# A convolution's taps moved from VectorE to ScalarE and accumulating DMA transfers, in a gated matmul kernel on one core

## The chip, the core and the metric

The kernel runs on one core of a Trainium2 chip. The metric is the device time of one execution in microseconds (us). A profile of one execution names the engines as PE (TensorE, with PEld for its weight loads), DVE (VectorE), ACT (ScalarE), POOL (GpSimd) and SP (SyncE, which here only issues DMA transfers).

## What is computed

```python
# x (8, 4096, 192), weight (8, 7), w_in (192, 2048), w_out (2048, 192), all float32
w = softmax(weight, axis=-1)                   # 8 heads of 24 columns, 7 taps
x_pad = concatenate([zeros(B, 6, D), x], axis=1)
conv[b, s, col] = sum_k w[head(col), k] * x_pad[b, s + k, col]
h = conv.reshape(32768, 192) @ w_in
g = h * (1 / (1 + exp(-1.702 * h)))
out = g @ w_out                                # (32768, 192)
```

## The kernel before

**Batches and steps.** The eight sequences are two halves of four. A batch (`big`, 0 to 31) is 512 tokens of one sequence of each half. It lies with 64 rows of d_model on the lower 64 partitions for the batch's first 256 tokens and on the upper 64 for the second 256. Each batch is done in two steps s = 2 big and s = 2 big + 1, 64 steps in all. Steps 0 and 1 are written out (`first_step`, `second_step`), steps 2 to 63 are one loop of `hidden`, `give`, `output`.

**What a batch needs beforehand (`prepare`, L432).** `transpose_x` (L385) has DVE turn the loaded tile xin into xt, three instructions. `load_x` (L103) then loads the next batch's x by eight transfers on SP's queue. `conv` multiplies each of three chunks c of 64 columns by its seven taps k: k = 0 is a multiply (L400), k = 1 to 6 a multiply-add onto f (L402), all on DVE over 128x512. `sums_c` (L310, L312) makes eight sums V1 to V8 of the chunks' quarters, because the products follow a fast scheme that multiplies sums. `cross` (L410) copies f to the other 64 partitions (`crossed`) by DMA on SP's queue: for the even step in three parts (V1 and its neighbour first, 128 KB; the quarters, 256 KB; V2 to V8, 448 KB), for the odd step in one of 832 KB.

**Where that work stands.** `prepare` yields pieces with an estimated time. They wait in the list `todo`, and calls of `work(us)` at fixed places in `hidden` and `output` take as many of them as fit, so that DVE does them between what PE and ACT wait for. `need(label)` takes all up to a label. Each engine works through its instructions in the order in which the program writes them.

**A step.** `hidden` (L490) makes 21 terms of the first matmul by `product1` (L457: 64 rows by 128 columns, 256 tokens) in four PSUM tiles: `sums` and the slots x, z and y. ACT copies some partial sums out into five SBUF tiles `kept` of 128x1024, called k15, k16, k19, k18 and k20 (L498, L503, L509, L511, L517), DVE adds and subtracts, and ACT applies the gelu (L473) into g. `fetch` puts term 16 of the next step into z ahead of the last two terms of this one; it needs V1 and its crossing. `output` (L603) makes the products p1, p2, p6, p5 and p7 by `product2` (L547, 64 matmuls each, 128 rows by 32 columns) and four short ones (L563). Between them ACT copies results out of PSUM (L611 and L612 after p1, L618 after p2, L624 after p6, L631 and L633 after p5, L640 after p7). DVE makes sums of g (L483) and of the results, and turns them (L581), and SP stores them (L596). While `output` runs, all five `kept` tiles are free.

**Buffers that matter.** f has two buffers, xin and xt one each, `kept` five that live for the whole run. The slots are PSUM tiles of two banks: a bank can be written again once its readers are done.

Of the kernel before, what the change touches and what calls it, by code (L numbers as in the profile page):

```python
# [15 lines left out]
def kernel(  # L16
# [73 lines left out]
    def load_x(big):  # L90


        p, c = divmod(big, CHUNKS)
        xin = xins[big] = xin_pool.tile([P, 2, NJ, XW], F32, name="xin")
        if c == 0:
            nc.gpsimd.memset(xin[0:R, :, 0, :], 0.0)
        for n in range(2):
            for o in range(2):
                j = 1 if c == 0 and o == 0 else 0
                t = c * TOK + o * T + (j - 1) * Q  # L100
                for v in range(2):
                    q0 = o * R + v * Q
                    nc.sync.dma_start(  # L103
                        out=xin[q0 : q0 + Q, n, j:NJ, :],
                        in_=x_v[n, p, t : t + (NJ - j) * Q, v * Q : v * Q + XW].rearrange(
                            "(j i) d -> i j d", i=Q
                        ),
                    )
# [272 lines left out]
    def transpose_x(big, c, n=None):  # L381
        if big not in xts:
            xts[big] = xt_pool.tile([P, NC, 2, XT], F32, name="xt")
        ns = slice(0, 2) if n is None else slice(n, n + 1)
        vec.transpose(  # L385
            xts[big][:, c, ns, :].rearrange("p n (j t) -> p (n j) t", t=Q),
            xins[big][:, ns, :, :].rearrange("p n j d -> p (n j) d")[:, :, c * R : c * R + Q],
        )
        if c == NC - 1 and n != 0:
            xins.pop(big)  # L390

    def conv_src(big, c, k, ns=slice(0, 2)):
        return xts[big][:, c, ns, Q - PAD + k : Q - PAD + k + T]
# [12 lines left out]
    def sums_c(big, i):  # L406
        add_up(lambda j: fs[big][:, j, :], *SUMS_C[i])
# [12 lines left out]
    def cross_even(*what):  # L420
        if given[0] < what[0] - 1:
            waiting.append(what)
        else:
            cross(what[0], 0, *what[1:])
# [7 lines left out]
    def prepare(big):  # L432

        for c in range(NC):
            yield "", 0.7, lambda c=c: transpose_x(big, c)
        if big + 1 < N_BIG:
            yield "", 0.0, lambda: load_x(big + 1)
        yield "", 0.0, lambda: new_f(big)

        for c in (0, 2):  # L440
            for k in range(K):
                yield "", 0.76 if k else 0.48, lambda c=c, k=k: conv(big, c, k)
        yield "", 0.38, lambda: sums_c(big, 0)
        yield f"first {big}", 0.0, lambda: cross_even(big, V1, C32 + 1)
        for k in range(K):
            yield "", 0.76 if k else 0.48, lambda k=k: conv(big, 1, k)
        yield "", 0.0, lambda: cross_even(big, 0, V1)
        for i in range(1, len(SUMS_C)):
            yield "", 0.38, lambda i=i: sums_c(big, i)
        yield f"all {big}", 0.0, lambda: cross_even(big, C32 + 1, NB)  # L450

    def product1(slot, a, b, s, first=False):
        f, o = fs[s // 2], s % 2
        for j in range(2):
            for h in range(2):

                nc.tensor.matmul(  # L457
                    slot[:, h, j * T : (j + 1) * T],
                    w_in_s[halves[h], a, j * P : (j + 1) * P],
                    (f if h == o else crossed)[halves[h], b, :],  # L460
                    start=(first and j == 0),
                    stop=True,
                    skip_group_check=True,
                )
# [14 lines left out]
    def sum_g(u, dst):  # L479
        j = NK // 2 * u  # L480
        v = [g[:, b, j : j + NK // 2, :] for b in range(NS)]
        a, b = {T1: (B12, B11), T2: (B22, T1), T3: (B22, B12), T4: (T2, B21)}[dst]
        vec.tensor_sub(v[dst], v[a], v[b])  # L483
# [6 lines left out]
    def hidden(s, x, z, y, work, fetch):  # L490

        k15, k16, k19, k18, k20 = kept

        def pe(slot, *ts, first=False):
            terms(s, slot, *ts, first=first)

        pe(sums, 12)
        act.copy(k15, sums)  # L498
        pe(x, 5, 17)
        gelu(B11, 0, x)  # L500
        pe(z, 7, first=True)
        pe(sums, 0)
        act.copy(k16, sums)  # L503
        work(1.5)
        pe(y, 6, 14, first=True)
        vec.tensor_sub(x, z, k15)
        work(2.6)
        pe(sums, 13)
        act.copy(k19, sums)  # L509
        pe(x, 2)  # L510
        act.copy(k18, x)  # L511
        pe(z, 11)
        pe(sums, 20, 10)
        vec.tensor_sub(k15, y, k19)  # L514
        gelu(B12, 0, sums)
        pe(x, 4)
        act.copy(k20, x)  # L517
        vec.tensor_sub(k19, z, k19)
        work(1.1)
        gelu(B22, 1, k19)  # L520
        gelu(B22, 0, k15)
        pe(y, 8)
        pe(sums, 1, 9, first=True)
        pe(y, 15)
        sum_g(0, T1)
        work(1.1)
        vec.tensor_add(k20, k20, sums)  # L527
        vec.tensor_sub(k16, y, k16)
        gelu(B11, 1, k20)
        pe(x, 18)  # L530
        gelu(B21, 1, x)
        gelu(B21, 0, k16)
        sum_g(0, T2)
        fetch()
        pe(sums, 3, 19)
        work(0.7)
        vec.tensor_add(k18, k18, sums)  # L537
        gelu(B12, 1, k18)
        work(1.1)
# [60 lines left out]
    def chunk(t, c):  # L600
        return t[c * Q : (c + 1) * Q, :]

    def output(s, ra, rb, work, between=None):  # L603

        out = Out(s)
        u1, u2, p3, p4 = (
            u_pool.tile([NC * Q, T], F32, name=f"u{i}") for i in range(4)
        )

        p1, p3c = product2(ra, 0, (A11, B11), (S4, B22, 0))  # L610
        act.copy(u1, p1)  # L611
        act.copy(chunk(p3, 0), p3c)  # L612
        sum_g(1, T1)
        sum_g(1, T2)
        sum_g(1, T4)
        sum_g(0, T4)
        p2, p3c = product2(rb, 0, (A12, B21), (S4, B22, 1))
        act.copy(chunk(p3, 1), p3c)  # L618
        vec.tensor_add(u2, u1, p2)  # L619
        out.turn(0, 0, u2)  # L620
        sum_g(0, T3)
        sum_g(1, T3)
        p6, p3c = product2(ra, 1, (S2, T2), (S4, B22, 2))
        act.copy(chunk(p3, 2), p3c)  # L624
        vec.tensor_add(u2, u1, p6)
        work(4.2)
        if between:
            between()
        p5, p4c = product2(rb, 1, (S1, T1), (A22, T4, 0))
        q = quarters(rb, 0, A22, T4, 2)  # L630
        act.copy(chunk(p4, 0), p4c)  # L631
        vec.tensor_add(u1, u2, p5)
        act.copy(chunk(p4, 2), q[2])  # L633
        vec.tensor_add(p3, u1, p3)
        out.turn(0, 1, p3)
        for l in (0, 1, 3):
            vec.tensor_add(chunk(p4, 2), chunk(p4, 2), q[l])
        work(1.5)
        p7, p4c = product2(ra, 0, (S3, T3), (A22, T4, 1))
        act.copy(chunk(p4, 1), p4c)  # L640
        vec.tensor_add(u1, u1, p7)
        vec.tensor_add(u2, u2, p7)
        out.turn(1, 1, u1)
        vec.tensor_sub(u2, u2, p4)
        out.turn(1, 0, u2)
        out.store()
# [143 lines left out]
    def second_step(fetch):  # L790

        quarters = [
            (0, 0, slots[2], B11), (1, 0, sums, B21), (1, 1, slots[0], B22), (0, 1, slots[1], B12)
        ]
        for u in range(2):
            for i, (m, n, slot, b) in enumerate(quarters):
                plain(1, u, m, n, slot)
                gelu(b, u, slot)
                if u == 1 and i < 2:
                    sum_g(0, (T1, T2)[i])  # L800
                work(2.5)
        todo.extend(("", 0.42, lambda i=i: sums_w_in(i)) for i in range(FREE, len(SUMS_W)))
        todo.append(("sums", 0.0, lambda: None))
        todo.extend(prepare(2))
        output(1, slots[0], slots[1], work, fetch)
        need("all 1")
        cross(1, 1)
        need("sums")
# [4 lines left out]
    def fetch(s, slot):  # L813

        need(f"first {s // 2}")
        terms(s, slot, 16, first=True)
# [8 lines left out]
    second_step(fetch_2)  # L825
    for s in range(2, N_ST):
        more = s + 1 < N_ST
        hidden(s, x, z, y, work, lambda: fetch(s + 1, z) if more else None)
        give(s)
        if more:  # L830
            begin(z)
        if s % 2 and (s + 3) // 2 < N_BIG:
            todo.extend(prepare((s + 3) // 2))
        output(s, y, x, work)
        if s % 2 and more:
            need(f"all {(s + 1) // 2}")
            cross((s + 1) // 2, 1)
        x, z = z, x
# [30 lines left out]
```

## Time and profile before

| | |
|---|---|
| time, median of 3 runs | 2382.21 us (2382.08 to 2382.79) |
| span of the profiled execution | 2380.8 us, 71620 instructions |
| multiply-adds of taps (L402) on DVE, 128x512 | 558, 747 ns each, 416.9 us |
| first taps (L400) on DVE, 128x512 | 93, 466 ns each, 43.4 us |
| turning of x (L385) on DVE, 128x576 | 93, 744 ns each, 64.8 us |
| copies to k15, k16, k19 (ACT, 128x1024) | 62 of each, 1012 ns each |
| copies of 32 or 96 rows by 256 in the output (ACT) | 364 to 369 ns |
| copies of 128x512 from PSUM (ACT, at the start) | 592 and 586 ns |
| transfers on SP's queue | 131.06 MB, 28.2% of 16 engines' time |
| transfers issued by POOL | one, 0.13 MB |

A line of the page's fifth part, or of the list of groups, gives line, engine, operation, output and input tiles, shapes and count; then the busy time, the mean of one, and the idle time of the engine just before with what ended it. A line of the timeline gives start and length in us, engine and line, and in brackets the wait before it. A line of the DMA issues gives the queue, the count, the size of one and the time from issue to landing. In the granted clock PE has full speed all the time.

### The profile page before, as it was taken

The page shows a single profiled execution, that of the slowest core. Times are in us where ns is not written, and L with a number is a line of the kernel's source. Part 1 is how long each engine was busy: PE and PEld are TensorE (multiplying, and loading weights), DVE is VectorE, ACT ScalarE, POOL GpSimd, SP SyncE. Part 2 cuts the span into 40 slices and gives each one's busy share as a digit, 9 for nine tenths or more (in the row PEclk, how much of TensorE's full clock was granted, in tenths as well). Part 3 has the DMA queues.
Part 4 walks back from the last instruction along what each step waited for, and adds up shares of the span by engine and source line. Part 5 has one row for each costly group of instructions (what it writes and reads, how often), then busy time and mean ns, then how long its engine had stood idle before and what let it go on. Part 6 is the DMA issues. An engine that isn't in the chain of part 4 may idle for free.

```text
span 2380.8 us, 71620 instructions
## 1 busy us (share of the span) xinstructions
PE 2371.0 (100%) x32598; PEld 1748.3 (73%) x32598; DVE 2038.6 (86%) x2855; ACT 1051.4 (44%) x1363; POOL 9.0 (0%) x30
## 2 busy tenths in 40 slices
PE   9999999999999999999999999999999999999998
PEld 6777777777777777777777777777777777777776
DVE  8898988888888889888898888898888988889865
ACT  5345344344453443444534434445344344453443
POOL 1000000000000000000000000000000000000000
PEclk9999999999999999999999999999999999999999
DMA  7323323223233132331232322323313233123120
GB/s 165 71 50 58 65 53 66 48 42 69 50 68 59 30 68 56 62 65 36 56 67 52 66 51 41 69 50 67 59 30 68 58 61 66 39 52 68 25 42 15
DMA packets 195983, 136.02 MB, mean 57 GB/s; under 512 B 110784, under 2 KB 186176, under 8 KB 193696
## 3 DMA queue, kind: packets, MB, share of 16 engines
q1 hardware_dynamic: 194912, 131.06, 28.2%
q8 instruction: 255, 4.18, 0.7%
q10 hardware_dynamic: 720, 0.26, 0.1%
q14 instruction: 48, 0.39, 0.1%
q0 software_dynamic: 48, 0.13, 0.0%
HBM read 53.15 MB, written 25.17 MB: 33 GB/s over the span
## 4 chain that ended last, share of the span: by engine, by line
PE 99%; DMA 1%; ACT 0%; DVE 0%; SPq 0%; issue 0%; ACTq 0%; DVEq 0%
PE slot L547 47%; PE slot L457 28%; PE sums L457 21%; PE slot L563 2%; DMA g<-in_moe_w_in_dram 0%; DMA crossed<-f 0%; SPq L103 0%; DVE f L291 0%; ACT f L281 0%; ACT kept L281 0%; ACT f L280 0%; ACT kept L280 0%; ACT f L282 0%; DVE osb L581 0%; SPq L227 0%
## 5 line engine op out<-in xcount | busy, mean ns | idle before, releaser
L547 PE MATMUL slot<-g,w_out_s 128*32 128x256 f32 x20544 | 1133.5, 379 | 0.0
L547 PEld LDWEIGHTS slot<-g,w_out_s 128*32 128x32 f32 x20544 | 661.0, 110 | 451.2 <-issue 20.9
L457 PE MATMUL slot<-f,w_in_s 64*128 64x256 f32 x3120 | 724.7, 376 | 0.0
L457 PE MATMUL slot<-crossed,w_in_s 64*128 64x256 f32 x3120 | 724.6, 376 | 0.0
L483 DVE TENSOR_TENSOR g<-g 128x1024 f32<-128x1024 f32 x504 | 602.5, 1215 | 82.3 <-ACT g L473 77.0
L457 PEld LDWEIGHTS slot<-crossed,w_in_s 64*128 64x128 f32 x3120 | 583.1, 187 | 35.7 <-issue 0.4
L457 PEld LDWEIGHTS slot<-f,w_in_s 64*128 64x128 f32 x3120 | 583.1, 187 | 34.1 <-issue 0.8
L457 PE MATMUL sums<-crossed,w_in_s 64*128 64x256 f32 x2280 | 559.2, 379 | 0.9 <-DMA crossed<-f 0.9
L457 PE MATMUL sums<-f,w_in_s 64*128 64x256 f32 x2280 | 559.2, 379 | 0.0
L457 PEld LDWEIGHTS sums<-crossed,w_in_s 64*128 64x128 f32 x2280 | 421.3, 187 | 38.3 <-issue 12.8
L457 PEld LDWEIGHTS sums<-f,w_in_s 64*128 64x128 f32 x2280 | 421.3, 187 | 36.4 <-issue 12.8
L402 DVE SCALAR_TENSOR_TENSOR f<-xt,cw,f 128x512 f32<-128x512 f32 (+1 forms) x570 | 422.7, 742 | 14.4
L473 ACT ACTIVATE g<-kept 128x1024 f32<-128x1024 f32 x310 | 321.0, 1058 | 141.4 <-DVE kept L537 82.5
L473 ACT ACTIVATE g<-slot 128x1024 f32<-128x1024 f32 x136 | 138.3, 1017 | 52.2 <-PE slot L457 52.2
L631 ACT COPY u<-slot 32x256 f32<-32x256 f32 x63 | 23.2, 368 | 248.4 <-PE slot L563 248.4
L514 DVE TENSOR_TENSOR kept<-slot,kept 128x1024 f32<-128x1024 f32 x62 | 75.7, 1221 | 63.8 <-ACT kept L509 63.8
L527 DVE TENSOR_TENSOR kept<-kept,sums 128x1024 f32<-128x1024 f32 x62 | 75.7, 1221 | 55.9 <-PE sums L457 55.8
L581 DVE STREAM_TRANSPOSE osb<-u 96x256 f32<-96x256 f32 x253 | 111.2, 439 | 7.3 <-DVE u L619 0.5
L473 ACT ACTIVATE g<-sums 128x1024 f32<-128x1024 f32 x66 | 67.6, 1024 | 97.8 <-PE sums L457 97.8
L624 ACT COPY u<-slot 32x256 f32<-32x256 f32 x63 | 23.0, 365 | 194.4 <-PE slot L547 194.4
L509 ACT COPY kept<-sums 128x1024 f32<-128x1024 f32 x62 | 62.8, 1012 | 97.8 <-PE sums L457 97.8
L537 DVE TENSOR_TENSOR kept<-kept,sums 128x1024 f32<-128x1024 f32 x62 | 75.7, 1221 | 27.3 <-PE sums L457 24.3
(112 smaller groups left out, 1347.0 us busy)
## 6 DMA issues: line engine op xcount, KB each, us to landing
xin<-in_x_dram SPq DMA_DIRECT2D x240, 180.0 KB, 5.0
crossed<-f SPq DMA_DIRECT2D x31, 832.0 KB, 5.8
out_dram<-osb SPq DMA_DIRECT2D x382, 64.0 KB, 1.9
crossed<-f SPq DMA_DIRECT2D x31, 448.0 KB, 3.8
crossed<-f SPq DMA_DIRECT2D x31, 256.0 KB, 2.9
crossed<-f SPq DMA_DIRECT2D x31, 128.0 KB, 2.2
g<-in_moe_w_in_dram SPq DMA_DIRECT2D x8, 384.0 KB, 9.5
g<-in_moe_w_out_dram SPq DMA_DIRECT2D x4, 768.0 KB, 4.7
```

Source lines behind the costliest of these rows:

```text
L402: vec.scalar_tensor_tensor(out=dst, in0=src, scalar=tap, in1=dst, op0=ALU.mult, op1=ALU.add)
L457: nc.tensor.matmul(slot[:, h, j * T : (j + 1) * T], w_in_s[halves[h], a, j * P : (j + 1) * P], (f if h == o else crossed)[halves[h], b, :] ...
L473: act.activation(g[:, b, j : j + NK // 2, :].rearrange("p f t -> p (f t)"), src.rearrange("p h n -> p (h n)"), AF.Gelu_apprx_sigmoid,)
L483: vec.tensor_sub(v[dst], v[a], v[b])
L509: act.copy(k19, sums)
L514: vec.tensor_sub(k15, y, k19)
L527: vec.tensor_add(k20, k20, sums)
L537: vec.tensor_add(k18, k18, sums)
L547: nc.tensor.matmul(dst[l * Q : (l + 1) * Q, :], w_out_s[:, a, j, c * Q : (c + 1) * Q], g[:, b, j, :], start=(first and j == 0), stop=(j == ...
L563: nc.tensor.matmul(dst[l], w_out_s[:, a, j, c * Q : (c + 1) * Q], g[:, b, j, :], start=(i == 0), stop=(i == NK // 4 - 1), skip_group_check ...
L581: vec.transpose(self.osb[:, n, :, m * Q : (m + 1) * Q], src.rearrange("p (j t) -> p j t", t=Q),)
L631: act.copy(chunk(p4, 0), p4c)
```

## The change

From the batch of steps 4 and 5 on (big = 2), DVE no longer makes the convolution. It still turns x and makes the sums V1 to V8. The product of a tap with xt is made by ACT (`tap`). For k = 0 it is written to f; for k = 1 to 6 it goes to a "lot", one half of a `kept` tile, and POOL issues a DMA transfer that adds the lot to f in place (128 partitions by 512, 256 KB). The five tiles give ten lots; an eleventh is again the lot with index 2, the first half of the second tile, k16. The taps go k outermost, c innermost, so that three transfers lie between two that add to the same chunk at the same k and the next.

The 21 taps of a batch are spread over two outputs (`some_taps`): 2, 2, 3 and 3 in the output of the odd step, and 2, 2, 3 and 4 in that of the even step that follows. So the first has the three multiplies to f and seven lots, the second eleven lots. Each group stands behind ACT's copies from PSUM of one product.

`prepare` is split for these batches. `turns` (turn x, load the next) and `sums_of` (V1 to V8 and the crossings for the even step) both go into `todo` at the start of an odd step's `hidden`: `turns` for the batch whose taps start in that step's output, `sums_of` for the batch that starts with the next step. Before, all of `prepare` started behind the odd step's `hidden`. The purpose is to take the multiply-adds off DVE and give them to ACT and the DMA engines, which have more idle time.

```diff
--- before.py
+++ after.py
@@ -448,6 +448,46 @@
         for i in range(1, len(SUMS_C)):
             yield "", 0.38, lambda i=i: sums_c(big, i)
         yield f"all {big}", 0.0, lambda: cross_even(big, C32 + 1, NB)
+
+    def turns(big):
+
+        for c in range(NC):
+            yield "", 0.7, lambda c=c: transpose_x(big, c)
+        if big + 1 < N_BIG:
+            yield "", 0.0, lambda: load_x(big + 1)
+        yield f"turned {big}", 0.0, lambda: None
+
+    def sums_of(big):
+        yield "", 0.38, lambda: sums_c(big, 0)
+        yield f"first {big}", 0.0, lambda: cross_even(big, V1, C32 + 1)
+        yield "", 0.0, lambda: cross_even(big, 0, V1)
+        for i in range(1, len(SUMS_C)):
+            yield "", 0.38, lambda i=i: sums_c(big, i)
+        yield f"all {big}", 0.0, lambda: cross_even(big, C32 + 1, NB)
+
+
+
+    lots = [kept[j // 2][:, j % 2, :].rearrange("p (n t) -> p n t", n=2) for j in (*range(10), 2)]
+
+    def tap(big, c, k, lot):
+        dst = fs[big][:, 2 * c : 2 * c + 2, :]
+        act.mul(lot if k else dst, conv_src(big, c, k), cw[:, c, k : k + 1])
+        if k:
+            nc.gpsimd.dma_start(
+                out=dst.rearrange("p n t -> p (n t)"),
+                in_=lot.rearrange("p n t -> p (n t)"),
+                accum_op=ALU.add,
+            )
+
+    taps = []
+
+    def some_taps(n, used):
+        while n and taps:
+            big, c, k = taps.pop(0)
+            tap(big, c, k, lots[len(used)])
+            if k:
+                used.append(k)
+            n -= 1
 
     def product1(slot, a, b, s, first=False):
         f, o = fs[s // 2], s % 2
@@ -603,6 +643,10 @@
     def output(s, ra, rb, work, between=None):
 
         out = Out(s)
+        used = []
+        if s % 2 and (s + 3) // 2 < N_BIG:
+            need(f"turned {(s + 3) // 2}")
+            new_f((s + 3) // 2)
         u1, u2, p3, p4 = (
             u_pool.tile([NC * Q, T], F32, name=f"u{i}") for i in range(4)
         )
@@ -610,18 +654,21 @@
         p1, p3c = product2(ra, 0, (A11, B11), (S4, B22, 0))
         act.copy(u1, p1)
         act.copy(chunk(p3, 0), p3c)
+        some_taps(2, used)
         sum_g(1, T1)
         sum_g(1, T2)
         sum_g(1, T4)
         sum_g(0, T4)
         p2, p3c = product2(rb, 0, (A12, B21), (S4, B22, 1))
         act.copy(chunk(p3, 1), p3c)
+        some_taps(2, used)
         vec.tensor_add(u2, u1, p2)
         out.turn(0, 0, u2)
         sum_g(0, T3)
         sum_g(1, T3)
         p6, p3c = product2(ra, 1, (S2, T2), (S4, B22, 2))
         act.copy(chunk(p3, 2), p3c)
+        some_taps(3, used)
         vec.tensor_add(u2, u1, p6)
         work(4.2)
         if between:
@@ -631,6 +678,7 @@
         act.copy(chunk(p4, 0), p4c)
         vec.tensor_add(u1, u2, p5)
         act.copy(chunk(p4, 2), q[2])
+        some_taps(3 if s % 2 else 4, used)
         vec.tensor_add(p3, u1, p3)
         out.turn(0, 1, p3)
         for l in (0, 1, 3):
@@ -801,7 +849,8 @@
                 work(2.5)
         todo.extend(("", 0.42, lambda i=i: sums_w_in(i)) for i in range(FREE, len(SUMS_W)))
         todo.append(("sums", 0.0, lambda: None))
-        todo.extend(prepare(2))
+        todo.extend(turns(2))
+        taps.extend((2, c, k) for k in range(K) for c in range(NC))
         output(1, slots[0], slots[1], work, fetch)
         need("all 1")
         cross(1, 1)
@@ -825,12 +874,16 @@
     second_step(fetch_2)
     for s in range(2, N_ST):
         more = s + 1 < N_ST
+        if s % 2:
+            if (s + 3) // 2 < N_BIG:
+                todo.extend(turns((s + 3) // 2))
+                taps.extend(((s + 3) // 2, c, k) for k in range(K) for c in range(NC))
+            if (s + 1) // 2 < N_BIG:
+                todo.extend(sums_of((s + 1) // 2))
         hidden(s, x, z, y, work, lambda: fetch(s + 1, z) if more else None)
         give(s)
         if more:
             begin(z)
-        if s % 2 and (s + 3) // 2 < N_BIG:
-            todo.extend(prepare((s + 3) // 2))
         output(s, y, x, work)
         if s % 2 and more:
             need(f"all {(s + 1) // 2}")
```

## Prediction, made before the changed kernel was run

> **What bounds the kernel now.** I read the page's busy line first, then the chain of work that ended last, then that chain in order of time.
>
> ```profile
> PE 2371.0 (100%) x32598; PEld 1748.3 (73%) x32598; DVE 2038.6 (86%) x2855; ACT 1051.4 (44%) x1363; POOL 9.0 (0%) x30
> PE 99%; DMA 1%; ACT 0%; DVE 0%; SPq 0%; issue 0%; ACTq 0%; DVEq 0%
> ```
>
> ```profile
> 1186.02 13.95 PE slot L547 x256
> 1222.61 13.95 PE slot L547 x256
> 1259.21 13.95 PE slot L547 x256
> ```
>
> PE is busy all the time and is 99% of the chain. In the chain in order of time the first long product of an output comes every 36.6 us, to 0.01 us, in step after step. So no step waits for DVE, ACT or a DMA. Groups of matmuls follow at 0.21 to 0.22 us, and the PE order of the changed kernel is the same. So the DVE time saved has nothing to buy, and the question is only whether the change makes PE wait. That is read from the slack of ACT's copies, in ACT's timeline of one output and the hidden part after it:
>
> ```profile
> 1190.05 0.37 ACT L612 COPY u<-slot 32x256 f32<-32x256 f32 x1
> 1193.12 0.37 ACT L618 COPY u<-slot 32x256 f32<-32x256 f32 x1 [2.71 <-PE slot L547]
> 1196.58 0.36 ACT L624 COPY u<-slot 32x256 f32<-32x256 f32 x1 [3.09 <-PE slot L547]
> 1201.74 0.36 ACT L633 COPY u<-slot 32x256 f32<-32x256 f32 x1 [0.48 <-DVE u L632]
> 1204.35 0.37 ACT L640 COPY u<-slot 32x256 f32<-32x256 f32 x1 [2.24 <-PE slot L547]
> 1205.45 1.01 ACT L498 COPY kept<-sums 128x1024 f32<-128x1024 f32 x1 [0.73 <-PE sums L457]
> 1208.85 1.01 ACT L503 COPY kept<-sums 128x1024 f32<-128x1024 f32 x1 [0.70 <-PE sums L457]
> 1211.44 1.01 ACT L509 COPY kept<-sums 128x1024 f32<-128x1024 f32 x1 [1.58 <-PE sums L457]
> ```
>
> I set zero at 1185.94, where PE starts that output; steps repeat, so this ruler serves every step. The copies to k15, k16 and k19 (L498, L503, L509) start at 19.5, 22.9 and 25.5. PE's timeline says how late each may be: the next matmul that adds to the bank of k16's copy is term 13,
>
> ```profile
> 1210.36 0.38 PE L457 MATMUL sums<-f,w_in_s 64*128 64x256 f32 x1
> ```
>
> at 24.4. The copy takes 1.0 us, so it must start by 23.4: 0.5 us of slack. For k15 (next use at 1207.77) it is 1.3, for k19 0.5.
>
> [...] No accumulating transfer is in this trace. [...]
>
> **The change part by part.**
>
> *DVE, removed:* per batch of two steps, 18 multiply-adds at 747 ns (L402) and 3 multiplies at 466 ns (L400): 14.8 us of 73.2, 30 batches, 445 us in all. Worth nothing: no PE wait ended on them.
>
> *ACT, added:* 21 multiplies of 128x512. ACT's rows give 365 ns for 256 elements and 1012 for 1024, so 0.58 for 512; the 128x1024 activations that read SBUF take 0.04 longer than those from PSUM: 0.62, or 0.6 back to back. They stand behind the copies named above, where ACT waits 2.7, 3.1, 4.0 and 2.2 us for PE. Two take 1.2, three 1.8: hidden. The last four of an even step end at 16.2 + 2.4 = 18.6, where the L640 copy would start at 18.4. That is 0.2 us late, and the slot it frees is next written by PE at 22.7. Nothing.
>
> *Transfers, added:* 18 a batch, 540 in all, 256 KB each, issued by POOL in order. A transfer waits for the multiply, for the transfer three before it (same c), and for POOL. In an even step eleven are made: multiplies done at 5.1 and 5.7 (behind L612, which ends at 4.5), at 8.2 and 8.8 (behind L618), at 11.6, 12.2 and 12.8 (behind L624), at 16.8, 17.4, 18.0 and 18.6 (behind L633, which ends at 16.2). In chunk 2 the chain is k3 at 5.8, k4 at 11.6, k5 at 16.8, k6 at 18.6. The eleventh, (c 2, k 6), has its lot in kept1, the buffer of k16. So the L503 copy now waits until (2,6) has been read out; it can't start before (2,5) has landed. Call L the time from free to landed. Then (2,6) lands at 16.8 + 2L while L is under 5.2, at 11.6 + 3L up to 5.8, and at 5.8 + 4L above. Behind the waiting L503 stand all of ACT's gelus, and PE's term 13 waits for it: what exceeds 23.4 is PE idle, once in each of 30 even steps.
>
> *What L is.* The transfers of this trace:
>
> ```profile
> crossed<-f SPq DMA_DIRECT2D x31, 256.0 KB, 2.9
> crossed<-f SPq DMA_DIRECT2D x31, 128.0 KB, 2.2
> xin<-in_x_dram SPq DMA_DIRECT2D x16, 160.0 KB, 4.0
> crossed<-f ACTq DMA_DIRECT2D x2, 64.0 KB, 7.8
> crossed<-f POOLq DMA_DIRECT2D x1, 128.0 KB, 6.7
> ```
>
> From below: the SP crossings say 1.5 us fixed and 0.7 per 128 KB of 64 partitions. [...] From above: the one POOL transfer here took 6.7 us where SP's took 2.2, but while DMA was 86% busy; its extra 4.5 on top of 2.9 gives 7.4. I take L = 5.0, the middle: POOL's own issue (0.7 us in its timeline) and its wait for a semaphore come into each link, and the last links run beside the output's stores, which start 20.8 after zero. Then (2,6) lands at 26.8, and the stall is 26.8 - 23.4 = 3.4 us, times 30 = 102 us. The odd steps have seven transfers; with L = 5 the last, (0,3), lands at 23.9 (chain 8.8, 13.8, 18.8), before its buffer is wanted at 26.4 (L511): nothing.
>
> *Moved:* the x load (eight transfers, L103) and the sums V1 to V8 go into the odd step's hidden part. DVE turns x there from 21.6 on (where it ended the output's work), with L506 between: the load starts at 25.0, and the load in this trace moves its data in 8.1 us, to 33.1. V1 waits for (2,6) and is crossed by the same SP queue behind the load, about 0.8 us more: 33.9, where PE's fetch needs it at 33.9 (1219.86). So this wait is near zero or up to 1 us if the added transfers slow the load; but a PE that is already 3.4 late doesn't see it. Nothing on top. *Second step, once:* ten weight sums (0.37) and three turns (0.73) now stand ahead of the sums of g in its output, 5.9 us, where T2 had some 3.5 to 4 to spare: 2 us.
>
> Sum: 2382.2 + 102 + 2 = 2486.
>
> **The rivals.** *Not slower:* [...] (2,6) lands at 23.2, k16 is not held, the crossing just fits: 2382 to 2387. For it: the short times of the SP transfers and a mean DMA share of 28%. Against: POOL's 6.7. *A little slower:* L is 3.3 to 4.1, or the crossing is late by up to 1 us (30 us): 2387 to 2430. *Much slower:* the transfers need 6.0 us or more, as bandwidth or POOL's turn-round binds. At 6.0 (2,6) lands at 29.8, 6.4 late: 192 us, 2576; at 6.7 it is 32.6 and 9.2: 276 us, 2660. [...] *Faster:* only if the 0.3 to 0.4 us that PE's loads show as "issue" at the two changes of matmul shape in a step shrank; nothing touches them.
>
> **How the numbers follow.** L from 4.1 to 5.9: 0.58, and the number is its 2486. Not slower, within 0.2% (4.8 us): 0.11. A little slower: 0.14. Much slower: 0.15. Faster: 0.02. The range goes from 2381 to 2620 (L about 6.35): it leaves out the faster case and the upper two thirds of the much slower one, about 0.12. Slower in all: 0.87.
>
> **What would show it.** The profile after should have the first product of outputs at intervals of 36.6 and 40.0 in turn; the ACT copy to k16 waiting for a DMA of kept some 3.4 us in 30 steps, and PE or its loads waiting for that copy; DVE near 1600 us, ACT near 1430; the accumulates landing after 5 us, those of one c never overlapping. It is wrong if the intervals stay even (L short), if the wait is at the fetch with crossed as the source (the load), or if both parities of steps grow (bandwidth).

## The result and the profile after

| | before | changed |
|---|---|---|
| time, median of 4 runs | 2382.45 us (2382.08 to 2382.79) | 2566.14 us (2562.22 to 2568.67) |
| ratio | | 1.077, 95% interval 1.0754 to 1.0786 |
| PE busy / mean granted clock | 2371.0 us / 0.999 | 2435.8 us / 0.974 |
| DVE, ACT, POOL busy | 2038.6, 1051.4, 9.0 us | 1624.5, 1462.3, 484.2 us |
| median time to landing of an accumulate | none | 4.3 us, 540 of them |

The change costs 184 us, where 104 were predicted. Times are medians; a profile is of one execution, which lay up to 9 us above its kernel's median. The page of the changed kernel, its busy line and its chain:

```profile
PE 2435.8 (95%) x32598; PEld 1784.4 (70%) x32598; DVE 1624.5 (63%) x2225; ACT 1462.3 (57%) x1993; POOL 484.2 (19%) x570
...
PE 82%; DMA 11%; ACT 3%; issue 2%; POOL 1%; DVE 0%; SPq 0%; ACTq 0%; POOLq 0%; DVEq 0%
```

PE is no longer the whole chain: 11% of the span is DMA. And PE's own busy time has grown by 65 us, though it has the same 32598 matmuls. What ended the waits, in the list of waits of the changed kernel (us in total, times, longest):

```profile
ACT kept L543 <- DMA f<-kept: 159.8, 30, 7.8
...
PEld sums L497 <- ACT kept L543: 132.4, 30, 6.8
...
PE sums L497 <- ACT kept L543: 120.3, 30, 6.4
...
DVE f L312 <- DMA f<-kept: 99.5, 30, 6.6
```

L543 is ACT's copy to k16 (L503 before), L497 PE's first matmul (L457 before). Thirty times, once in every batch from the third on, that copy waits for an accumulate, and PE for the copy. The chain in order of time shows one such place, and what it adds to the interval between outputs (start, length, what):

```profile
1197.95 13.95 PE slot L587 x256
1234.55 13.95 PE slot L587 x256
1276.45 13.95 PE slot L587 x256
```

The interval behind an odd step's output (the first here) is 36.60 us as before; that behind an even step's is 41.90. Over the 30 batches the first kind stays at 36.60 and the second averages 42.81, which is 6.21 more; 30 x 6.21 = 186 us is the whole difference between the two profiled spans. Between 1234.55 and 1276.45 the same chain, seen closer, runs

```profile
1254.23 0.86 POOL f L476
1255.09 0.47 issue
1255.58 5.61 DMA f<-kept
1261.34 1.02 ACT kept L543
1262.36 0.04 issue
1262.41 1.92 PE sums L497 x8
1264.32 2.63 PE slot L497 x16
1266.95 1.73 PE sums L497 x16
```

The last accumulate of the batch is issued at 21.0 us after the output's start and takes 5.6; the copy follows at 26.8, and PE's term 13 at 27.9 instead of 24.4. Then come eight matmuls in 1.92 us, where sixteen take 1.73 a little later. (Counts of matmuls here are records of the trace; a call of L497 leaves two.) POOL's and ACT's timelines show the queue of the same place:

```profile
1251.69 0.87 POOL L476 DMA_DIRECT2D f<-kept  x1 [1.67 <-ACT kept L474]
1252.94 0.87 POOL L476 DMA_DIRECT2D f<-kept  x1 [0.38 <-ACT kept L474]
1254.23 0.87 POOL L476 DMA_DIRECT2D f<-kept  x1 [0.42 <-issue]
1255.58 0.87 POOL L476 DMA_DIRECT2D f<-kept  x1 [0.47 <-DMA f<-kept]
```

```profile
1250.68 2.56 ACT L474 ACTIVATE kept<-xt,cw 128x512 f32<-128x512 f32 x4
...
1261.34 1.01 ACT L543 COPY kept<-sums 128x1024 f32<-128x1024 f32 x1 [4.66 <-DMA f<-kept]
```

The fourth transfer of the group, for chunk 2 like the first, is issued only when the first has landed: 3.9 us from issue to issue. (Two transfers of the other chunks lie between two of the same chunk, not three as the description of the change has it.) The windows of the changed kernel around the restart show the second loss. The columns are the length, the busy time of PE, PEld, DVE, ACT and POOL with the count of instructions, then the granted clock, the DMA share and GB/s:

```profile
1254.00:1260.00 6.00, 5.06 (x48) 4.19 (x44) 4.68 (x9) 1.97 (x2) 1.74 (x2) 1.00 1.02 171
1260.00:1264.00 4.00, 1.59 (x8) 1.35 (x10) 2.03 (x5) 1.01 (x1) 0.00 (x0) 0.83 1.01 209
```

The granted clock is not 1.00 behind the wait. In the trace's record of the clock, PE has half speed from 1262.61 for 3.41 us. Such stretches follow 29 of the 30 waits, 20 of them 3.41 us long and 9 of 6.83, 129.7 us in all. Of that, 11.9 us still lie in the waits; of the rest half is lost, 58.9 us or 1.96 a batch. So the 6.21 us are 4.01 of idle PE, 1.96 of half clock and a rest of 0.24. A wait without half clock has such a rest too: with three copies, below, 1.47 us of idle PE lengthen the interval by 1.74. The traces don't show what it is; it is called the restart here. The DMA share is 1.01 to 1.02 in both windows, so full DMA engines are a rival to be tested.

### The profile page after: what moved, and what is told of

Its sections match the earlier page's. It is cut to its first block, busy times and chain, and to the rows that moved or that the text cites. A ratio compares the mean times of both kernels' runs of the same rounds, so it can differ in the third digit from the quotient of the medians.

```text
span 2567.0 us, 73597 instructions
## 1 busy us (share of the span) xinstructions
PE 2435.8 (95%) x32598; PEld 1784.4 (70%) x32598; DVE 1624.5 (63%) x2225; ACT 1462.3 (57%) x1993; POOL 484.2 (19%) x570
## 3 DMA queue, kind: packets, MB, share of 16 engines
q0 software_dynamic: 77808, 141.72, 32.9%
## 4 chain that ended last, share of the span: by engine, by line
PE 82%; DMA 11%; ACT 3%; issue 2%; POOL 1%; DVE 0%; SPq 0%; ACTq 0%; POOLq 0%; DVEq 0%
PE slot L587 39%; PE slot L497 22%; PE sums L497 19%; DMA f<-kept 10%; PE slot L603 2%; ACT kept L474 1%; ACT kept L543 1%; POOL f L476 1%; DMA g<-in_moe_w_in_dram 0%; DVE u L679 0%; ACT u L678 0%; DMA crossed<-f 0%; ACT kept L538 0%; SPq L103 0%; ACTq L543 0%
## 5 line engine op out<-in xcount | busy, mean ns | idle before, releaser
L476 POOL DMA_DIRECT2D f<-kept x540 | 475.6, 962 | 1944.2 <-ACT kept L474 1723.3
L497 PE MATMUL slot<-f,w_in_s 64*128 64x256 f32 x3120 | 760.5, 390 | 0.0
L497 PE MATMUL slot<-crossed,w_in_s 64*128 64x256 f32 x3120 | 760.5, 390 | 0.0
L497 PE MATMUL sums<-crossed,w_in_s 64*128 64x256 f32 x2280 | 586.0, 392 | 122.1 <-ACT kept L543 120.3
L497 PEld LDWEIGHTS slot<-crossed,w_in_s 64*128 64x128 f32 x3120 | 609.8, 196 | 48.7 <-issue 0.4
L497 PEld LDWEIGHTS slot<-f,w_in_s 64*128 64x128 f32 x3120 | 609.7, 196 | 34.3 <-issue 0.4
L497 PE MATMUL sums<-f,w_in_s 64*128 64x256 f32 x2280 | 586.0, 392 | 0.0
L497 PEld LDWEIGHTS sums<-crossed,w_in_s 64*128 64x128 f32 x2280 | 432.7, 193 | 176.1 <-ACT kept L543 132.4
L497 PEld LDWEIGHTS sums<-f,w_in_s 64*128 64x128 f32 x2280 | 432.7, 193 | 36.4 <-issue 12.3
L474 ACT ACTIVATE kept<-xt,cw 128x512 f32<-128x512 f32 x540 | 353.7, 712 | 3.8
L543 ACT COPY kept<-sums 128x1024 f32<-128x1024 f32 x62 | 62.8, 1012 | 183.6 <-DMA f<-kept 159.8
L312 DVE TENSOR_TENSOR f<-f 128x256 f32<-128x256 f32 x186 | 73.2, 421 | 101.7 <-DMA f<-kept 99.5
L567 DVE TENSOR_TENSOR kept<-kept,sums 128x1024 f32<-128x1024 f32 x62 | 75.7, 1221 | 77.3 <-PE sums L497 75.7
L549 ACT COPY kept<-sums 128x1024 f32<-128x1024 f32 x62 | 62.8, 1012 | 108.6 <-PE sums L497 108.6
```

The lines of the kernel that those rows point to most:

```text
L312: vec.tensor_sub(v(dst), v(a), v(b))
L474: act.mul(lot if k else dst, conv_src(big, c, k), cw[:, c, k : k + 1])
L476: nc.gpsimd.dma_start(out=dst.rearrange("p n t -> p (n t)"), in_=lot.rearrange("p n t -> p (n t)"), accum_op=ALU.add,)
L497: nc.tensor.matmul(slot[:, h, j * T : (j + 1) * T], w_in_s[halves[h], a, j * P : (j + 1) * P], (f if h == o else crossed)[halves[h], b, :] ...
```

## The experiments

Theory A: the copy to k16 waits until the last accumulate out of k16's buffer has landed (5.6 us after its issue in the place above); PE's wait is paid in its own length and, if it is long, in a stretch at half clock behind it. Theory B: the DMA engines are too full; whatever buffer is used, the same time goes. Theory C: the lower clock comes from the added traffic, not from PE's waiting. All intervals in brackets are those of the ratio to the kernel before.

### A wait of known length, without any transfer

In the kernel before, the copy to k16 is repeated in the odd steps 3 to 61.

```diff
-        act.copy(k16, sums)
+        for _ in range(3 if s % 2 and s < N_ST - 1 else 1):   # 5, 4 in the others
+            act.copy(k16, sums)
```

Three copies:

> The kernel before (convolution on DVE, no accumulating transfers) with ACT's copy to k16 made three times instead of once in the odd steps 3 to 61, the same data each time. A copy every 1.0 to 1.1 us puts the end of the third at 22.9 + 3.1 to 3.3 = 26.0 to 26.2 after an output's start, where PE's term 13 is due at 24.4: PE idles 1.6 to 1.8 us, 30 times, 48 to 54 us. Theory A (a wait of PE costs its own length, and in addition a while at half clock behind it if the wait is long, 3 us and more): 1.7 us is too short, 2431 to 2437 us, granted clock 1.0 throughout. Theory B (any wait drops the clock): 1.7 to 2.2 us more each time, 2480 to 2500. Theory C (the drop of the clock in the changed kernel comes from its DMA traffic, not from the wait): 2431 to 2437 here and in the longer dose.

Five copies:

> The same with five copies instead of one: the last ends at 28.0 to 28.4, so PE idles 3.6 to 4.0 us, 30 times, 108 to 120 us, as long as in the changed kernel (4.0 on average). Theories A and B: a stretch at half clock follows each wait as in the changed kernel, 1.7 to 2.2 us more each, 51 to 65 us: 2541 to 2567 us, though not one transfer was added. Theory C: 2490 to 2502, clock 1.0.

Four copies, run later than the two:

> The dose between: four copies to k16 instead of one in the odd steps 3 to 61 of the kernel before. Three copies gave 1.47 us of idle PE and no half clock, five 3.56 us and one stretch of 3.4 us at half clock (1.71 us lost) each time. Four should give 2.5 us of idle, 30 times, and 2.8 us on the interval for the wait alone: 2466 us. If the clock drops only from about 3 us of idle on: 2464 to 2470. If what counts is how much of a fixed stretch of 3.4 us is idle, so that the moment of the wait decides, part of the 30 waits are followed by a half-clock stretch: 2475 to 2510.

| copies | time | ratio | PE idle at each wait | waits followed by half clock |
|---|---|---|---|---|
| 3 | 2434.42 | 1.0219 (1.0204 to 1.0234) | 1.47 us | 0 of 30 |
| 4 | 2492.76 | 1.0461 (1.0445 to 1.0477) | 2.51 us | 15 of 30 |
| 5 | 2543.20 | 1.0675 (1.0657 to 1.0692) | 3.56 us | 30 of 30 |

Theory C falls: five copies, with no transfer added, give the half clock. The chain in order of time of the kernel with five copies, behind one wait, and its windows around the same place:

```profile
1254.23 2.08 PE sums L457 x8
...
1295.17 1.73 PE sums L457 x16
```

```profile
1250.50:1254.00 3.50, 0.17 (x2) 0.00 (x0) 0.17 (x1) 3.41 (x4) 0.00 (x0) 0.98 0.67 140
1254.00:1257.50 3.50, 3.27 (x16) 2.71 (x18) 0.10 (x1) 1.19 (x2) 0.00 (x0) 0.53 0.02 5
1257.50:1261.00 3.50, 3.50 (x34) 3.07 (x34) 2.35 (x2) 1.66 (x2) 0.00 (x0) 1.00 0.00 0
```

PE stands still in the first window; in the second it works, with 16 matmuls where the third has 34, at a clock of 0.53. The DMA share is 0.02 then.

The dose of four decides how the clock falls. All its waits are 2.51 us long, yet every second one is followed by half clock, in strict turn. Two neighbours in the windows of that kernel:

```profile
1226.00:1229.50 3.50, 0.99 (x10) 0.56 (x8) 0.80 (x2) 3.18 (x4) 0.00 (x0) 1.00 0.65 131
1229.50:1233.00 3.50, 3.50 (x34) 3.15 (x36) 1.35 (x2) 1.93 (x2) 0.00 (x0) 1.00 0.18 37
1302.00:1305.50 3.50, 0.99 (x10) 0.56 (x8) 0.78 (x2) 3.16 (x4) 0.00 (x0) 1.00 0.65 130
1305.50:1309.00 3.50, 3.50 (x22) 2.94 (x22) 1.23 (x1) 1.86 (x2) 0.00 (x0) 0.62 0.18 37
```

So the length alone does not decide. In the changed kernel's record of the clock the stretches at half clock are 3.413 us long or 6.827, and behind the waits each starts 78.51, 81.92 or 153.60 us after the one before: 23, 24 and 45 times 3.4133. Two batches of this run, 73.2 + 2.78 and 73.2 + 4.47, are 153.65 us, again 45 times 3.413 (153.6), so each pair of waits lies in nearly the same places on a grid of that period.

What decides, as far as the traces tell, is how much of a wait falls into one period of this grid. This is read from them afterwards; no run was made for it. In each kernel that has several half-clock stretches, they all start on one grid of 3.4133 us, to within 0.002 us (where there is one alone, it sets the grid). Laid over PE's idle time in the twelve traces, the grid gives: whenever PE idled for more than 1.94 us of a period, half clock came with the next one; under 1.84 us it never did; of the seven periods from 1.84 to 1.94 two brought it. (In the changed kernel's trace alone the least that brought it is 1.99 us, the most that did not 1.84.) The 2.51 us of this run fall now wholly or mostly into one period (2.02 us or more), now into two (at most 1.84 in one). A stretch once begun went on for a second period in the 12 cases in which PE idled for 0.62 us or more of the first one, and ended where it idled for 0.49 or less. With five copies the steps settle at 78.51 us for two, 23 periods, so nearly all waits lie in the same place; that each of the 30 brought half clock is in part due to this.

### Work in place of the idle time

PE gets 16 more matmuls (32 records of the trace, some 3.5 us) where it would wait, with weights of zero, onto y.

```diff
+    none = consts.tile([P, UW], F32)
+    nc.gpsimd.memset(none, 0.0)
     ...
         pe(y, 6, 14, first=True)
+        if s % 2 and s < N_ST - 1:
+            for i in range(8):
+                for h in range(2):
+                    nc.tensor.matmul(y[:, h, i % 2 * T : (i % 2 + 1) * T],
+                        none[halves[h], i % 2 * P : (i % 2 + 1) * P],
+                        (fs[s // 2] if h == s % 2 else crossed)[halves[h], 0, :],
+                        start=False, stop=True, skip_group_check=True)
```

With the five copies:

> The same five copies, but in those steps PE gets 16 more matmuls (as four more terms) with weights of zero, added onto y while it would wait: 3.5 us of work that changes no result. Theories A and B: PE hardly idles, the clock stays at 1.0, and the time falls to the wait alone: 2490 to 2504 us, some 50 to 60 us less than without the extra work. Theory C, or if the drop doesn't depend on PE being idle: no gain over the run without the extra matmuls.

Measured: 2498.33 us, 1.0487 (1.0471 to 1.0502). PE is left 0.11 us of idle at a wait, no half-clock stretch remains (the mean granted clock is 0.999, 0.979 without the added work), and the kernel is 45 us faster than the one with the same wait and less work.

In the changed kernel:

> The changed kernel with the same 16 zero-weight matmuls ahead of term 13 in the odd steps 3 to 61. Its waits for k16's lot average 4.0 us (3.1 to 6.4), so 3.5 us of work fits in nearly all of them. Theories A and B: half-clock stretches gone or nearly so, time 2382 + 30 x 4.0 to 4.4 = 2502 to 2515 us, 50 to 64 us faster than the changed kernel with more PE work in it. Theory C: 2566 as before, or more.

Measured: 2513.47 us, 1.0547 (1.0531 to 1.0563), 53 us less than the changed kernel. One wait is still followed by a half-clock stretch; the mean granted clock is 0.998, 0.974 in the changed kernel. ACT waits for the accumulates as long as before (158.3 us in total). So of the 184 us some 53 go when PE works in the gap, as the half clock goes with it; some 131 stay: the wait itself, which PE now mostly spends on the added matmuls.

### The eleventh lot in a buffer of its own

```diff
-    lots = [... for j in (*range(10), 2)]
+    lots = [... for j in range(10)]
+    extra = consts.tile([P, 2 * T], F32)
+    lots.append(extra.rearrange("p (n t) -> p n t", n=2))
```

> The changed kernel with one thing undone: the eleventh lot of an even step has a buffer of its own (128x512) instead of the first half of k16. Same multiplies, same 540 transfers, same chain. Theory A (PE stalls because k16's copy waits for the last accumulate to have read its lot): that wait of 159.8 us in total is gone. Two smaller waits stand behind it: DVE's V1 still waits for the same transfer (landed 26.8 after an output's start) and holds DVE's next difference by about 2.4 us where PE has some 1.6 to spare, and the crossing of V1 is issued behind the load of x at 29.8 and lands 4 to 6.5 later, where PE's fetch wants it at 33.9: 1 to 2.5 us in all, 30 times, mostly at full clock: 2412 to 2460 us. Theory B (the DMA engines are too full: bandwidth, not the buffer): another wait takes its place in full, 2540 to 2570.

Measured: 2480.08 us, 1.0415 (1.0398 to 1.0433), 86 us less, but above what was expected. Theory B's number is not met; the wait of the copy to k16 is gone, and two others have come forward. From the waits of this kernel:

```profile
DVE f L312 <- DMA f<-extra: 101.3, 30, 7.2
...
PEld slot L499 <- DVE kept L556: 41.6, 29, 3.4
PEld slot L499 <- DMA crossed<-f: 40.6, 27, 2.9
```

DVE's V1 (L312) waits for the same accumulate and holds the difference behind it (L556), for which PE waits; later PE waits for V1's crossing. Each is some 1.4 us a batch. I had put the two together at 1 to 2.5 us; they are 2.7 in these rows, and 3.15 on the interval. In the changed kernel both lay behind the wait for k16.

### Ten lots

One tap goes to the odd step's output, so that no eleventh lot is needed.

```diff
-        some_taps(2, used)                       # behind p1
+        some_taps(3 if s % 2 else 2, used)
-        some_taps(3 if s % 2 else 4, used)       # behind p5
+        some_taps(3, used)
```

> The changed kernel with one tap moved from the even step's output (where it needed the eleventh lot) to the odd step's: 3, 2, 3, 3 taps there, and 2, 2, 3, 3 in the even one, ten lots. Same work, same transfers. The last accumulate of a batch is then free of a link: chain 2 goes at 8.9, 13, 18, lands at 22.5 to 23.5. Theory A: no wait for k16, no wait of V1; left is V1's crossing, queued behind the load of x, landing at 34 to 36 where the fetch is due at 33.9: 0 to 1.5 us, 30 times: 2382 to 2427 us, clock near 1.0. Theory B (bandwidth): 2500 and more, as the traffic is the same.

Measured: 2440.04 us, 1.0247 (1.0231 to 1.0262). The traffic is the same as in the changed kernel, so theory B falls: 126 of 184 us went by moving one multiply. (That other transfers lengthen a link, 3.9 us for one and 5.6 for the last above, is not excluded.) It is 13 us above my upper number. What is left is PE's wait for the crossing of V1, and one wait of 3.8 us in the last batch:

```profile
PEld slot L497 <- DMA crossed<-f: 40.8, 27, 2.8
...
PE slot L497 <- DMA crossed<-f: 30.0, 27, 2.4
```

### Ten lots, and the load of x behind the sums

```diff
     def turns(big):
         ...
-        if big + 1 < N_BIG:
-            yield "", 0.0, lambda: load_x(big + 1)
     def sums_of(big):
         ...
         yield f"all {big}", 0.0, lambda: cross_even(big, C32 + 1, NB)
+        if big + 2 < N_BIG:
+            yield "", 0.0, lambda: load_x(big + 2)
     ...
         todo.extend(turns(2))
+        todo.append(("", 0.0, lambda: load_x(3)))
```

> Ten lots as in the run before, and the load of the next x is issued behind V1 to V8 and their crossings instead of ahead of them. Theory A: no wait of PE left, 2380 to 2386 us, the time of the kernel before, with DVE at about two thirds of the span: the change itself then costs nothing and brings nothing. If time is left above 2390, a wait that I have not named remains. Theory B: 2500 and more.

Measured: 2389.71 us, 1.0029 (1.0018 to 1.0040): no wait for the crossing is left. The 128 KB crossing, from the DMA issues of the kernel with ten lots and of this one:

```profile
crossed<-f SPq DMA_DIRECT2D x31, 128.0 KB, 6.1
```

```profile
crossed<-f SPq DMA_DIRECT2D x31, 128.0 KB, 2.2
```

It stood behind eight transfers of 180 KB on its queue, and no longer does. The run missed my 2386 by 4 us, and the profile names most of it: in the last batch, which has no x to turn, V1 stands ahead of the difference that frees slot x, waits for its accumulate, and PE waits 3.8 us, once. No half clock follows this wait. The grid of 3.4133 us cuts it in two, 1.94 and 1.88 us of idle PE, and both periods, like the next, have full clock:

```profile
2271.60:2275.01 3.41, 1.47 (x14) 0.97 (x10) 0.93 (x3) 1.01 (x1) 0.00 (x0) 1.00 0.81 145
2275.01:2278.42 3.41, 1.53 (x14) 1.40 (x16) 3.38 (x8) 0.35 (x1) 0.00 (x0) 1.00 0.54 115
2278.42:2281.84 3.42, 3.42 (x36) 3.06 (x34) 2.35 (x3) 1.84 (x3) 0.00 (x0) 1.00 0.64 134
```

### The last named wait

```diff
             if (s + 3) // 2 < N_BIG:
                 ...
+            else:
+                todo.append(("", 1.5, lambda: None))   # V1 goes behind the difference
```

> Ten lots, the load behind the sums, and in the last batch (which has no x to turn) V1 behind the difference that frees slot x instead of ahead of it, where it made PE wait 3.8 us once in the run before. Theory A: the last named wait is gone, 2382 to 2386 us: the convolution on ACT and the DMA engines costs nothing, and it brings nothing either, since PE sets every interval. If more than 2387 is left, there is a cost that I haven't named.

Measured: 2385.31 us, 1.0013 (1.0007 to 1.0020). PE is busy for 2371.3 us, 2371.0 in the kernel before, with DVE at 1621 us of 2384. So the same multiplies and the same 540 transfers cost 3 us, of which PE waits of under 0.8 us for DVE (1.8 us in four places) are seen; the rest of the 3 us I did not trace. No version here is faster than the kernel before.

### Copies in place of additions

```diff
                 in_=lot.rearrange("p n t -> p (n t)"),
-                accum_op=ALU.add,
```

> The changed kernel with plain copies in place of the accumulating transfers, same sizes, queue, order and waits; left out is the addition, so f holds the last tap's product alone. Theory A1 [...]: a link falls from 4.3 to 3.3 to 3.7 us, the last lands at 23.8 to 24.8, PE idles 0.4 to 1.4 us 30 times, no half clock: 2394 to 2430 us. Theory A2 [...]: a link stays above 4.1, 2530 to 2566.

Measured: 2429.98 us, 1.0208 (1.0190 to 1.0226). The time to landing, in the DMA issues of the changed kernel and of this one:

```profile
f<-kept POOLq DMA_DIRECT2D x540, 256.0 KB, 4.3
```

```profile
f<-kept POOLq DMA_DIRECT2D x540, 256.0 KB, 2.6
```

A copy of the same bytes from the same queue lands in 2.6 us instead of 4.3: 1.7 us, 40% of an accumulate, come with the addition. So do 0.33 us of POOL's instruction (0.87 against 0.55), and the packets of POOL's queue fall from 77808 to 43248. The 2.6 us are below my 3.3 to 3.7. Yet the time is at the upper end of what I gave, because the copy to k16 still waits in 16 batches (34.8 us in total), and V1's crossing holds PE as with ten lots (15.9 us in PE's waits); four of the batches have half clock, where I had given none. The run separates copy from addition; what the added time is spent on it does not show.

## Why the prediction was right, and where it was off

The direction, the place and the range were right: slower, through one wait in each even step's wake, at the copy to k16, behind the chain of accumulates of chunk 2. By its steps:

- **PE bounds, so DVE's saving buys nothing.** Right. DVE's busy time fell by 414 us, and in the last version, where all that is moved, the time is the one before within 0.2%.
- **ACT's multiplies are hidden.** Right. They took 712 ns each, and two took 1.33 us and four 2.56 rather than 1.2 and 2.4. PE waited for none of them; its weight loads did once, for 0.4 us.
- **The landing at 26.8 and a stall of 3.4 us.** At the place shown the copy started at 26.8, by other links than mine: from the multiply's end at 16.8 some 4.2 us to the first landing, then 5.7 more, not twice 5.0. That they add up to my sum is chance. Over 30 batches PE's idle time was 4.01 us (3.05 to 6.44). The mechanism was right, and the term was 0.6 us too small: 18 us.
- **What a stall costs.** Here the sum lacked a term. I priced an idle PE at its own length. Behind 29 of the 30 waits the clock is halved for one or two stretches of 3.41 us, and that is 1.96 us a batch, 59 us; the restarts add 0.24 a batch, 7 us. The trace of before has a mean clock of 0.999, PE never stands still in its steady part, and the one stretch at half clock starts at 2377.4, behind PE's last matmul (2374.6); so I counted on full speed. This is the larger part of the miss: 59 of some 80 us.
- **Once, in the second step, 2 us.** Wrong: the first two intervals are 41.78 and 37.80 in both kernels. The ten weight sums and the turns did run ahead, but T1 and T2 then ended by 94.9, in time for p6, of which only the second half needs them.
- **Moving the x load costs nothing on top.** Right for this kernel, where PE was late anyway. As a cost by itself I put it at 0 to 1 us. With ten lots it showed 1.1 us of idle PE in 27 batches, and the interval there is 2 us longer, 58 us of the whole; 0.2 us of the difference is half clock, the rest is open.
- **The rivals.** "Much slower" through full DMA engines was given 2576 to 2660; the time fell just below, but not for that reason: with the same traffic, ten lots take 2440 and the last version 2385. "Not slower" would have needed links of 3.3 us at most (16.8 + 2 x 3.3 = 23.4), which no transfer by POOL had shown before; 3.3 was the shortest seen, 4.3 the median.
- **The range.** That it holds 2566 is partly luck. Its upper part stood for links of up to 6.35 us; the idle time measured asks for links of some 5.3 in my formula (an estimate from 4.01), and the clock, which filled the rest, was not in it.

With 4.01 for 3.4, 1.96 for the clock, 0.24 for the restart and nothing for the second step, the sum is 2382 + 30 x 6.21 = 2568; measured 2566, and 2569 in the profiled execution.

## What to carry to other kernels

In the kernel before PE was busy for 2371.0 of 2380.8 us and waited for others for 2.0 us, both times in the first 30; so 414 us less on DVE bought nothing. In a kernel whose trace shows the same, judge a change by the waits that it adds: list each buffer that it shares, and put the last use on its chain beside the first reuse. A transfer that reads a buffer held it here until it had landed (5.6 us after its issue in the place shown), and a chain of accumulates onto one tile was as long as its links together (3.9 us from one issue to the next, then 5.6 for the last); one multiply moved ahead was worth 126 us. Price a PE wait like these, of some 1.9 us or more, with the half clock that may follow it (here 1.96 us a batch).

## What the runs showed of the hardware that I had not expected

- The half clock follows PE's idle time, not traffic: none at 1.47 us, every second time at 2.51, every time at 3.56, one stretch of 3.41 us, two in one case. At the 3.05 to 6.44 us of the changed kernel it followed 29 of 30 waits, two stretches in 9 of them; the one without is of 3.21 us. The shortest wait with one was 1.84 us, with ten lots, and the longest without 3.82, split over two periods of the grid. The idle time inside one period, of 3.41 us, with a bound near 1.9, fits all of these. With a buffer of its own for the eleventh lot some 2.2 us of idle PE a batch are split over two waits, and only one of 30 batches has half clock.
- Sixteen matmuls in each wait that change no result made the changed kernel 53 us faster, and the kernel with five copies 45 us.
- An accumulate of 256 KB lands in 4.3 us (3.3 to 7.5), a copy issued in the same way in 2.6; POOL's instruction for it takes 0.87 us. The one transfer by POOL in the kernel before, 6.7 us in a full stretch, was a poor measure, and the 2.9 of my lower bound an estimate that no accumulate had shown; that the middle of the two bounds came near is chance in part.
